# Sums of weight blocks: from VectorE additions with a store and a reload to transfers that add into the tile

## The chip, the cores and the metric

The kernel runs on one core of a Trainium2 chip. The time is what one execution takes on the device, in microseconds (us); before the change the median of two runs is 708.54 us (708.47 and 708.6). The profile is of one execution, recorded by the hardware.

The names used below are: TensorE (PE, the matmuls), VectorE (DVE), ScalarE (ACT), GpSimd (POOL) and SyncE (SP, which here only issues transfers). SPq and ACTq are the queues of transfers that SyncE and ScalarE issue. "L695" is line 695 of the kernel before.

## The reference

Two branches work on the same normalised input of 2048 rows and 512 columns, and their results are combined.

```
x  = A_x;  xn = layernorm(x)
s  = attention(xn @ wqkv: 32 heads of 16, each row sees 8 rows, 2 apart) @ wo
z  = gelu(xn @ w_in);  z1 = z[:, :896];  z2 = layernorm(z[:, 896:])
g  = w_sp @ z2 + b_sp            # w_sp is 2048 x 2048: it mixes the rows
b  = (z1 * g) @ w_out
out = x + s * silu(b)
```

What matters here is the product of the mixing weight `w_sp` with `z2` (2048 x 896). It is in float32.

## The kernel before

**Float32 on TensorE.** Each operand is split in a high part (written by ScalarE, L183) and a low part, the rest (written by VectorE, L184). A product of two blocks is three matmuls: high by high, high by low, low by high (`three`, L695). A weight block of 128 x 512 is loaded into a `raw` tile (SyncE's queue, L160), of which there are four, and split into one of eight pairs of high and low tiles (`prep`).

**The stages.** In the order of TensorE: qkv products (to about 110 us), the first half of `w_in` (z1), the second half with the layernorm (z2, 227 to 295), the mixing (295 to 583), the products with `w_out` (to 660) and with `wo` (to the end). The attention runs on VectorE in eight groups of heads. It has the lowest priority, so its steps are put wherever VectorE would have a gap, from z1 on to shortly before the products with `wo`.

**The mixing.** The output rows come in four groups of 512, called c. For c = 2 and 3 (295 to 447 us) all 16 blocks of `w_sp` are multiplied with `z2` as they are (line `PE g L695`). For c = 0 and 1 a scheme with fewer products is used on 3 of the 7 column blocks on either side (7 block products in place of 8): differences and sums of blocks of `z2` (`combine`, kept in `t_d`) are multiplied with sums of weight blocks. The seven are p1, p2, q6, q7, q5, q3 and q4, in this order, each by `block_product` over eight weight blocks, in four pairs. The middle column block (the "odd" one) is done without the scheme, beside p1, p2, q7 and q4. With `w[c, s]` for the block of output group c and input block s, and HT = 8, the sums are

- q6: `w[0,s] + w[1,s] + w[1,HT+s]`
- q7: `w[0,s] + w[1,s]`
- q5: `w[1,s] + w[1,HT+s]`
- q3: `w[0,s] + w[0,HT+s] + w[1,s] + w[1,HT+s]`

p1, p2 and q4 take a block as it is. Between the pairs of a product stand steps (`steps=`): loads and splits of the operands (`operand`: tiles `tr`), gate products (`upper_first` and others: `zl`) and splits of gated blocks of c = 2 and 3 (`late`: `ul`).

**Where the sums come from.** `block_sums(i)`, L557 to L569, makes all four for one s: two loads of 512 KB each (tiles `sa` and `sb`, L559 and L560), four additions on VectorE (L567), two stores of 512 KB into `sums_d` (L568 and L569, ScalarE's queue). It is called for i = 0 to 2 in the z1 loop and for i = 3 to 7 in the mixing of c = 2 and 3. q6, q7, q5 and q3 then load a block of sums like any other.

**What sets the order.** The kernel is written as a program in the order of the stages. The order of the instructions on each engine, except of those that are pinned to program order (the loads by L160 and the splits are), is chosen when it is built, by a scheduler which plays a model of the engines through. On the chip each engine works its own list in that order and waits, by semaphores, for what the next instruction needs. The transfers of one queue are issued in order too.

Of the kernel before, what the change touches and what calls it, by code (L numbers as in the profile page):

```python
# [11 lines left out]
F32 = mybir.dt.float32  # L12
F32R = mybir.dt.float32r
AF = mybir.ActivationFunctionType
ALU = mybir.AluOpType
AX = mybir.AxisListType

P = 128
# [6 lines left out]
FB = FH // P  # L25
NG = 3
CT = 512
NC = S // CT
JC = NT // NC
HT = NT // 2  # L30
# [16 lines left out]
RAW = 4  # L47
# [7 lines left out]
def kernel(  # L55
# [13 lines left out]
    nc = tc.nc  # L69
    pins = [True]  # L70

    def pin(ins):
        return tc.keep_in_program_order(ins) if pins[0] else ins
# [9 lines left out]
    raws = ctx.enter_context(tc.tile_pool(name="raws", bufs=1, side="right"))  # L83
# [3 lines left out]
    dram = ctx.enter_context(tc.tile_pool(name="scratch", bufs=1, space=DR))  # L87
# [3 lines left out]
    b_d = dram.tile([HT, P, 2, D], F32, name="b_d")  # L91
    z1_d = dram.tile([FB, NC, P, CT], F32, name="z1_d")
    g_d = dram.tile([2, FB, P, CT], F32, name="g_d")
    sums_d = dram.tile([2, HT, P, 2, CT], F32, name="sums_d")
    t_d = dram.tile([2, HT, P, 2, F3], F32, name="t_d")
    mv_d = dram.tile([NT, 2, P], F32, name="mv_d")
    o_d = dram.tile([NSUB, NT // NJ, CS, P // Q, NJ * Q], F32, name="o_d")
# [48 lines left out]
    def mm(name):  # L146
        return ps.tile([P, 512], F32, tag=f"bank{next(turn)}", name=name)
# [3 lines left out]
    def weight_pair(name):  # L151
        i = next(slot)
        return (
            wts.tile([P, 512], F32R, tag=f"whi{i}", name=name + "h"),
            wts.tile([P, 512], F32R, tag=f"wlo{i}", name=name + "l"),
        )

    def fetch(src, n, name):
        raw = raws.tile([P, 512], F32, tag="raw", name=name + "r", bufs=RAW)
        pin(nc.sync.dma_start(raw[:, :n], src))  # L160
        return raw

    def prep(src, n, name, raw=None):
        if raw is None:
            raw = fetch(src, n, name)
        hi, lo = weight_pair(name)
        split(hi[:, :n], lo[:, :n], raw[:, :n])
        return hi, lo

    @contextmanager  # L170
# [11 lines left out]
    def split(hi, lo, src):  # L182
        first_ = pin(nc.scalar.activation(hi, src, AF.Copy))  # L183
        pin(nc.vector.tensor_tensor(lo, src, hi.bitcast(F32), op=ALU.subtract))  # L184
        return first_
# [285 lines left out]
    def t4(name, n=2):  # L471
        t = wide.tile([P, 2 * CT], F32, tag="t4", name=name, bufs=WIDE)
        return t.rearrange("p (i t) -> p i t", i=2)[:, :n]
# [80 lines left out]
    for sub in range(NSUB):  # L554
        attention(sub)

    def block_sums(i):  # L557
        top, low = t4(f"sa_{i}"), t4(f"sb_{i}")
        nc.sync.dma_start(top, w_sp[0:2, i].rearrange("c p t -> p c t"))  # L559
        nc.sync.dma_start(low, w_sp[0:2, HT + i].rearrange("c p t -> p c t"))  # L560
        for out_, a, b in (
            (low[:, 1], top[:, 1], low[:, 1]),
            (top[:, 1], top[:, 0], top[:, 1]),
            (top[:, 0], top[:, 0], low[:, 1]),
            (low[:, 0], top[:, 0], low[:, 0]),
        ):
            nc.vector.tensor_tensor(out_, a, b, op=ALU.add)  # L567
        nc.scalar.dma_start(sums_d[0, i], top)  # L568
        nc.scalar.dma_start(sums_d[1, i], low)  # L569

    for f in range(FB):
        wh, wl = prep(w_in1[:, f, :], KB * P, f"w1_{f}")
        for c in range(NC):
            pz = mm(f"z1_{f}_{c}")
            for k in range(KB):
                cc = slice(k * P, (k + 1) * P)
                xh, xl = [planes[:, FB - KB + k, c * JC : (c + 1) * JC, a] for a in range(2)]
                nc.tensor.matmul(pz, wh[:, cc], xh, start=k == 0, stop=False)  # L578
                nc.tensor.matmul(pz, wh[:, cc], xl, start=False, stop=False)  # L579
                nc.tensor.matmul(pz, wl[:, cc], xh, start=False, stop=k == KB - 1)  # L580
            if c % 2 == 0:
                zp = t4(f"z1t_{f}_{c}")
            zt = zp[:, c % 2]
            if c == 0:
                nc.vector.tensor_tensor(zt, pz, rb, op=ALU.mult)
                pz = zt
            nc.scalar.activation(zt, pz, AF.Gelu_apprx_tanh)  # L587
            if c % 2:
                nc.scalar.dma_start(z1_d[f, c - 1 : c + 1].rearrange("c p t -> p c t"), zp)
        if f % 2:  # L590
            block_sums(f // 2)

    HALF = (slice(0, 512), slice(512, FH))
    WID = (512, FH - 512)
# [16 lines left out]
    def spatial_block(c, js):  # L611
        return prep(w_sp[c, js], CT, f"wsp_{c}_{js}")
# [55 lines left out]
    def bias(c):  # L668
        t = t4(f"bb_{c}")
        nc.sync.dma_start(  # L670
            t, b_sp[c : c + 2, :].rearrange("c t -> (c t)").unsqueeze(0).to_broadcast([P, 2 * CT])
        )
        return t
# [19 lines left out]
    def three(pg, z, w, start=False, stop=False, seeded=False):  # L693
        for i, (a, b) in enumerate(((0, 0), (0, 1), (1, 0))):
            nc.tensor.matmul(  # L695
                pg, z[a], w[b], start=start and i == 0, stop=stop and i == 2, skip_group_check=seeded
            )

    def z2_block(j, f):
        return [planes[:, f, j, a] for a in range(2)]  # L700
# [16 lines left out]
    for c in (2, 3):  # L717
        for n, js in enumerate(order):
            w = spatial.get((c, js)) or spatial_block(c, js)
            for f in range(FB):  # L720
                key = c, f
                three(banks[key], z2_block(js, f), w, n == 0 and key not in seeds, n == NT - 1, key in seeds)
            if n == HT:
                if c == 2:
                    banks[3, 0] = mm("g_3_0")
                else:
                    b01 = bias(0)
                    seed(("p", 0), "p1_0", b01[:, 0])
            if c == 2 and n % 4 == 0 or c == 3 and n == 5:
                block_sums(3 + n // 4 if c == 2 else 7)  # L730
        for f0 in range(0, FB, 2):
            n = min(2, FB - f0)
            zl = z1_pair(c, f0, n)
            gts = None if (c, f0 + n - 1) in seeds and f0 else t4(f"gt_{c}_{f0}", n)
            for f in range(f0, f0 + n):
                zt, src = zl[:, f - f0], banks[c, f]
                if (c, f) not in seeds:
                    gt = gts[:, f - f0]
                    nc.vector.tensor_tensor(gt, src, bb[:, c - 2], op=ALU.add)
                    src = gt  # L740
                nc.vector.tensor_tensor(zt, src, zt, op=ALU.mult)
                if c == 2 and f < FB - 1:
                    seed((3, f + 1), f"g_3_{f + 1}", bb[:, 1])
                if c == 3 and f < 3:
                    key = ("p", f + 1) if f < 2 else ("o", 0)
                    seed(key, f"p1_{f + 1}", b01[:, 0])
            nc.scalar.dma_start(g_d[c - 2, f0 : f0 + n].rearrange("f p t -> p f t"), zl)
# [11 lines left out]

    def block_product(name, key, z, w, odd=None, start=True, steps=()):  # L760
        for n, s0 in enumerate(range(0, HT, 2)):
            pair_ = [(s, prep(w(s), CT, f"{name}_{s}")) for s in (s0, s0 + 1)]
            for f in range(3):
                for s, wp in pair_:
                    three(
                        banks[key, f], z(s, f), wp, start and s == 0, s == HT - 1, not start
                    )
            if odd:
                for s, wp in pair_:
                    three(banks["o", odd[0]], odd[1](s), wp, False, s == HT - 1, True)  # L770
            for do in steps[n] if steps else ():
                do()
# [33 lines left out]
    def later(fn, *args):  # L806
        return lambda: fn(*args)
# [27 lines left out]

    T1, T2, T3, T4 = [[later(operand, i, h, s0) for s0 in range(0, HT, 2)] for i, h in ((0, 0), (1, 1), (1, 0), (0, 1))]

    block_product("p1", "p", upper, lambda s: w_sp[0, s], (0, odd_upper), start=False)
    ya, yb = t4("ya"), t4("yb")
    oq = t4("oq")  # L840
    yv, o1 = [ya[:, 0], ya[:, 1], yb[:, 0]], oq[:, 0]
    with urgent(400):
# [2 lines left out]
        nc.scalar.activation(o1, banks["o", 0], AF.Copy)  # L845
    nc.vector.tensor_tensor(b01[:, 1], b01[:, 0], b01[:, 1], op=ALU.add)
    block_product(
        "p2", "p", lower, lambda s: w_sp[0, HT + s], (0, odd_lower), start=False,
        steps=([], [T2[0]], [T2[1]], [T2[2]]),
    )  # L850
    fresh("q", "q6")
    block_product(
        "q6", "q", turned, lambda s: sums_d[0, s, :, 0],
        steps=(
            [T2[3], later(upper_first, 0)],
            [T3[0], later(upper_first, 2)],
# [6 lines left out]
    for f in range(3):  # L863
        seed(("q", f), f"q7_{f}", b01[:, 1], -1.0)
    seed(("o", 1), "o2", b01[:, 1])
    block_product(
        "q7", "q", turned, lambda s: sums_d[0, s, :, 1], (1, odd_upper), start=False,
        steps=([T3[3]], [T1[0]], [T1[1]], [T1[2], later(late, 2, 4, 1)]),
    )
    va, vb = t4("va"), t4("vb")  # L870
# [1 line left out]
    for f in range(3):  # L872
        minus(vv[f], yv[f], banks["q", f])
    fresh("q", "q5")
    block_product(
        "q5", "q", turned, lambda s: sums_d[1, s, :, 1],
        steps=([T1[3]], [later(late, 2, 5, 2)], [], []),
    )
    qv = [va[:, 1], vb[:, 1], oq[:, 1]]
    with urgent(400):  # L880
        for f in range(3):
            nc.scalar.activation(qv[f], banks["q", f], AF.Copy)
    block_product(
        "q3", "q", lambda s, f: z2_block(HT + s, FB - 3 + f), lambda s: sums_d[1, s, :, 0], start=False,
        steps=([T4[0], later(lower_last, 4, 2)], [T4[1], later(lower_last, 6, 1)], [T4[2]], [T4[3]]),
    )
    fresh("q4", "q4")
    block_product(
        "q4", "q4", turned, lambda s: w_sp[1, HT + s], (1, odd_lower), start=True,
        steps=(  # L890
            [later(upper_last, 4, 2)],
            [later(upper_last, 6, 1)],
# [23 lines left out]
    for i, j in enumerate(rows_of):  # L916
        c, jj = divmod(j, JC)
# [98 lines left out]
```

## Time and profile before

| | |
|---|---|
| median of 2 runs | 708.54 us |
| profiled execution: span | 706.6 us |
| runs' median less this span | 1.9 us |
| TensorE busy | 700.7 us (99% of the span) |
| VectorE busy | 619.2 us (88%) |
| ScalarE busy | 260.9 us (37%) |
| GpSimd busy | 41.8 us (6%) |
| moved by transfers | 151.93 MB, mean 215 GB/s |

The span goes from the first to the last instruction of the profiled execution; the time of a run has some more around it. The chain of waits is the work that ended last, followed back from the last instruction, at each step to what released it. A group of instructions is given with the number of them (x), the busy time and the mean of one. In the view of one tile it is the shortest, median and longest duration in ns. In the timeline each row has its start and its duration in us and, in square brackets, how long the engine was idle before it and what released it. Buffer numbers are left out of the tile names, so `q_4l` between 470 and 491 us is the low part of block 4 of q6, and `q_6r` the raw tile of a block 6.

### The profile page before, as it was taken

To read this page: it belongs to the slowest core of one execution; us is meant where nothing else is said; L and a number is where in the kernel's file an instruction comes from. 1 tells how busy PE (TensorE), PEld (TensorE's weight loads), DVE (VectorE), ACT (ScalarE), POOL (GpSimd) and SP (SyncE) were. 2 spreads that over 40 slices of the span, in tenths; PEclk is the share of its full clock that TensorE was granted. 3 is DMA by queue.
4 is the path that set the end of the run, shared out by engine and by line. 5 is a ranking of instruction groups with operands and counts; after the bars stand their busy time and mean duration, and the time that the engine had idled before them with its cause. 6 is when DMAs were issued, how large, how long until landed. Compare 5 with 4: busy or idle time off the path is not lost.

```text
span 706.6 us, 8920 instructions
## 1 busy us (share of the span) xinstructions
PE 700.7 (99%) x3152; PEld 585.4 (83%) x3152; DVE 619.2 (88%) x770; ACT 260.9 (37%) x403; POOL 41.8 (6%) x81
## 2 busy tenths in 40 slices
PE   8999999999999999999999999999999999999997
PEld 7888888888888988888888888888888888888886
DVE  6774599989998899989999999999999999799665
ACT  4343332343224466751112211354545542131531
POOL 3100000000000443320000000000000000000000
PEclk9999999999999999999999999999999999999999
DMA  8767775585785131579956742877857781353996
GB/s 271 255 189 228 240 242 178 161 287 207 258 275 220 33 135 69 190 255 323 328 183 219 288 135 60 307 239 260 276 200 269 246 260 59 125 165 101 303 327 235
DMA packets 96652, 151.93 MB, mean 215 GB/s; under 512 B 8672, under 2 KB 50912, under 8 KB 96608
## 3 DMA queue, kind: packets, MB, share of 16 engines
q1 hardware_dynamic: 57968, 108.77, 47.1%
q10 hardware_dynamic: 38640, 42.60, 17.3%
q8 instruction: 24, 0.39, 0.2%
q14 instruction: 20, 0.16, 0.1%
HBM read 100.40 MB, written 50.94 MB: 214 GB/s over the span
## 4 chain that ended last, share of the span: by engine, by line
PE 98%; DMA 1%; DVE 0%; SPq 0%; issue 0%
PE g L695 22%; PE q L695 12%; PE p L695 6%; PE qkv L371 6%; PE qkv L373 6%; PE qkv L372 6%; PE z L608 4%; PE z L607 4%; PE z L606 4%; PE z L580 4%; PE b L911 4%; PE z L578 4%; PE b L910 4%; PE b L912 4%; PE z L579 4%; PE s L911 2%
## 5 line engine op out<-in xcount | busy, mean ns | idle before, releaser
L503 DVE TENSOR_TENSOR pr<-k,q 128x2048 f32<-128x2048 f32 x32 | 73.2, 2286 | 1.9 <-DMA q<-qkv_d 1.5
L530 DVE TENSOR_TENSOR pv<-v,lg 128x2048 f32<-128x2048 f32 x32 | 73.3, 2291 | 0.9
L506 DVE TENSOR_REDUCE lg<-pr 128x128 f32<-128x2048 f32 x32 | 73.0, 2281 | 0.4
L391 ACT ACTIVATE stage<-qkv 128x512 f32<-128x512 f32 x36 | 21.4, 596 | 49.2 <-PE qkv L373 49.1
L536 DVE TENSOR_TENSOR pv<-pv 128x1024 f32<-128x1024 f32 x32 | 39.1, 1221 | 0.5
L608 PE MATMUL z<-w_0h,BIG 128*128 128x512 f32 x64 | 25.0, 391 | 0.0
L607 PE MATMUL z<-w_0l,BIG 128*128 128x512 f32 x64 | 25.0, 391 | 0.0
L606 PE MATMUL z<-w_0h,BIG 128*128 128x512 f32 x64 | 24.9, 389 | 0.0
L921 ACT ACTIVATE bt<-b 128x512 f32<-128x512 f32 x16 | 9.4, 597 | 41.5 <-PE b L912 41.5
L627 ACT ACTIVATE zt<-zt,nmz,mvz 128x896 f32<-128x896 f32 x16 | 17.9, 1134 | 17.6 <-POOL nmz L623 17.3
L267 DVE TENSOR_TENSOR xT<-xT,mr 128x512 f32<-128x512 f32 x20 | 13.8, 688 | 11.2 <-DMA mr<-mv_d 6.6
L537 DVE TENSOR_TENSOR pv<-pv 128x512 f32<-128x512 f32 x32 | 22.0, 687 | 0.6
L608 PE MATMUL z<-w_1h,BIG 128*128 128x384 f32 x64 | 21.5, 336 | 0.0
L606 PE MATMUL z<-w_1h,BIG 128*128 128x384 f32 x64 | 21.5, 335 | 0.0
L607 PE MATMUL z<-w_1l,BIG 128*128 128x384 f32 x64 | 21.4, 335 | 0.0
L587 ACT ACTIVATE z1t<-z 128x512 f32<-128x512 f32 x21 | 12.5, 594 | 21.8 <-PE z L580 21.8
L965 DVE TENSOR_TENSOR sg<-s,sg 128x512 f32<-128x512 f32 (+1 forms) x17 | 11.2, 657 | 10.6 <-PE s L912 9.7
L618 DVE BATCH_NORM_STATS2 zst<-zt 128x6 f32<-128x448 f32 x32 | 19.1, 610 | 1.5 <-ACT zt L609 1.5
L620 POOL TENSOR_TENSOR nmz<-mvz,mone 128x1 f32<-128x1 f32 x16 | 5.0, 315 | 234.8 <-DVE mvz L619 234.7
L184 DVE TENSOR_TENSOR BIG<-zt,BIG 128x896 fp32r<-128x896 f32 x16 | 17.1, 1079 | 1.1 <-ACT BIG L183 1.1
L609 ACT ACTIVATE zt<-z 128x512 f32<-128x512 f32 (+1 forms) x24 | 12.8, 535 | 13.4 <-PE z L608 12.1
L373 PE MATMUL qkv<-wqkv_0h,BIG 128*128 128x512 f32 x43 | 16.7, 389 | 0.0
(543 smaller groups left out, 2164.1 us busy)
## 6 DMA issues: line engine op xcount, KB each, us to landing
qkv_d<-stage ACTq DMA_DIRECT2D x24, 512.0 KB
k<-qkv_d SPq DMA_DIRECT2D x8, 960.0 KB
v<-qkv_d SPq DMA_DIRECT2D x8, 960.0 KB
z_d<-z1t ACTq DMA_DIRECT2D x14, 512.0 KB
t_d<-zt ACTq DMA_DIRECT2D x16, 384.0 KB
zl<-z_d SPq DMA_DIRECT2D x12, 512.0 KB
tr<-t_d SPq DMA_DIRECT2D x16, 384.0 KB
x<-in_x SPq DMA_DIRECT2D x16, 256.0 KB
```

The lines of the kernel that those rows point to most:

```text
L371: nc.tensor.matmul(pq, xh[:, k], wh, start=k == 0, stop=False)
L372: nc.tensor.matmul(pq, xh[:, k], wl, start=False, stop=False)
L373: nc.tensor.matmul(pq, xl[:, k], wh, start=False, stop=k == KB - 1)
L503: nc.vector.tensor_tensor(pr, taps(kw, j0), qb.unsqueeze(1).to_broadcast([P, W, NJ * CS]), op=ALU.mult)
L506: nc.vector.tensor_reduce(lg[:, :, j0 * HS : (j0 + NJ) * HS], pr.rearrange("p w (i d) -> p w i d", d=DH), axis=AX.X, op=ALU.add,)
L530: nc.vector.tensor_tensor(pr.rearrange("p w (i d) -> p w i d", d=DH), taps(vw, j0).rearrange("p w (i d) -> p w i d", d=DH), lg[:, :, j0 * ...
L536: nc.vector.tensor_tensor(pr[:, 0:4], pr[:, 0:4], pr[:, 4:8], op=ALU.add)
L606: nc.tensor.matmul(pz, xh[:, k], wh, start=k == 0, stop=False)
L607: nc.tensor.matmul(pz, xh[:, k], wl, start=False, stop=False)
L608: nc.tensor.matmul(pz, xl[:, k], wh, start=False, stop=k == KB - 1)
L695: nc.tensor.matmul(pg, z[a], w[b], start=start and i == 0, stop=stop and i == 2, skip_group_check=seeded)
L911: nc.tensor.matmul(pp[:, cols], hi, wl, start=False, stop=False)
```

## The change

`block_sums` and `sums_d` go, with the calls. `prep_sum` takes a list of blocks: the first is loaded into the raw tile by SyncE's queue, and each of the others is added to it by a transfer which GpSimd's queue issues with `accum_op=ALU.add`. After that the tile is split as before. p1, p2 and q4 have lists of one block. Compared with `prep`, the load and the split are no longer both pinned: the load in `prep_sum` isn't, the split is.

```diff
-    sums_d = dram.tile([2, HT, P, 2, CT], F32, name="sums_d")
...
+    def prep_sum(srcs, name):
+        hi, lo = weight_pair(name)
+        raw = raws.tile([P, 512], F32, tag="raw", name=name + "r", bufs=RAW)
+        nc.sync.dma_start(raw, srcs[0])
+        for src in srcs[1:]:
+            nc.gpsimd.dma_start(raw, src, accum_op=ALU.add)
+        split(hi, lo, raw)
+        return hi, lo
...
-    def block_sums(i):
-        top, low = t4(f"sa_{i}"), t4(f"sb_{i}")
-        nc.sync.dma_start(top, w_sp[0:2, i].rearrange("c p t -> p c t"))
-        nc.sync.dma_start(low, w_sp[0:2, HT + i].rearrange("c p t -> p c t"))
-        for out_, a, b in (
-            (low[:, 1], top[:, 1], low[:, 1]),
-            (top[:, 1], top[:, 0], top[:, 1]),
-            (top[:, 0], top[:, 0], low[:, 1]),
-            (low[:, 0], top[:, 0], low[:, 0]),
-        ):
-            nc.vector.tensor_tensor(out_, a, b, op=ALU.add)
-        nc.scalar.dma_start(sums_d[0, i], top)
-        nc.scalar.dma_start(sums_d[1, i], low)
...
-        if f % 2:
-            block_sums(f // 2)
...
-            if c == 2 and n % 4 == 0 or c == 3 and n == 5:
-                block_sums(3 + n // 4 if c == 2 else 7)
...
-            pair_ = [(s, prep(w(s), CT, f"{name}_{s}")) for s in (s0, s0 + 1)]
+            pair_ = [(s, prep_sum(w(s), f"{name}_{s}")) for s in (s0, s0 + 1)]
...
-    block_product("p1", "p", upper, lambda s: w_sp[0, s], (0, odd_upper), start=False)
+    block_product("p1", "p", upper, lambda s: [w_sp[0, s]], (0, odd_upper), start=False)
...
-        "q6", "q", turned, lambda s: sums_d[0, s, :, 0],
+        "q6", "q", turned, lambda s: [w_sp[0, s], w_sp[1, s], w_sp[1, HT + s]],
...
-        "q7", "q", turned, lambda s: sums_d[0, s, :, 1], (1, odd_upper), start=False,
+        "q7", "q", turned, lambda s: [w_sp[0, s], w_sp[1, s]], (1, odd_upper), start=False,
...
-        "q5", "q", turned, lambda s: sums_d[1, s, :, 1],
+        "q5", "q", turned, lambda s: [w_sp[1, s], w_sp[1, HT + s]],
...
-        "q3", "q", lambda s, f: z2_block(HT + s, FB - 3 + f), lambda s: sums_d[1, s, :, 0], start=False,
+        "q3", "q", lambda s, f: z2_block(HT + s, FB - 3 + f), lambda s: [w_sp[0, s], w_sp[0, HT + s], w_sp[1, s], w_sp[1, HT + s]], start=False,
```

p2 and q4 are changed as p1 is.

More of the change, by code (lines that the diff above doesn't have):

```diff
@@ L847 @@
     block_product(
-        "p2", "p", lower, lambda s: w_sp[0, HT + s], (0, odd_lower), start=False,
+        "p2", "p", lower, lambda s: [w_sp[0, HT + s]], (0, odd_lower), start=False,
         steps=([], [T2[0]], [T2[1]], [T2[2]]),
@@ L888 @@
     block_product(
-        "q4", "q4", turned, lambda s: w_sp[1, HT + s], (1, odd_lower), start=True,
+        "q4", "q4", turned, lambda s: [w_sp[1, HT + s]], (1, odd_lower), start=True,
         steps=(
```

## The prediction

> **What bounds the kernel now.** I read the head and the chain of waits first, then the busy time by stretch.
>
> ```profile
> span 706.6 us, 8920 instructions
> PE 700.7 (99%) x3152; PEld 585.4 (83%) x3152; DVE 619.2 (88%) x770; ACT 260.9 (37%) x403; POOL 41.8 (6%) x81
> PE 98%; DMA 1%; DVE 0%; SPq 0%; issue 0%
> ```
>
> TensorE is busy for 700.7 of 706.6 us and is 98% of the chain. Whatever is taken from another engine can win back at most 706.6 − 700.7 = 5.9 us, under 1%. The change can lose much more, wherever a weight block comes later than TensorE wants it. The stretches that use the sums are q6, q7, q5 and q3, with q4 behind them; the first two rows are stretches in which the sums are made (columns: stretch, its us, then busy us and instructions of PE, PEld, DVE, ACT, POOL, the granted clock, the DMA share, GB/s):
>
> ```profile
> 61.00:227.00 166.00, 166.00 (x740) 138.17 (x739) 141.98 (x137) 57.78 (x93) 0.00 (x0) 1.00 0.69 230
> 295.00:447.00 152.00, 152.00 (x673) 125.81 (x672) 144.16 (x169) 36.83 (x54) 6.62 (x14) 1.00 0.67 230
> 491.00:507.00 16.00, 16.00 (x72) 13.27 (x71) 16.00 (x19) 9.83 (x17) 0.00 (x0) 1.00 0.75 237
> 507.00:529.00 22.00, 22.00 (x98) 18.22 (x98) 22.00 (x28) 9.78 (x15) 0.00 (x0) 1.00 0.64 215
> 529.00:545.00 16.00, 16.00 (x72) 13.23 (x72) 15.09 (x18) 7.80 (x14) 0.00 (x0) 1.00 0.83 294
> 545.00:561.00 16.00, 16.00 (x72) 13.24 (x71) 16.00 (x24) 9.72 (x17) 0.00 (x0) 1.00 0.72 230
> 561.00:583.00 22.00, 22.00 (x99) 18.21 (x98) 21.25 (x32) 10.87 (x19) 0.00 (x0) 1.00 0.81 257
> ```
>
> From 491 on VectorE is as full as TensorE, since attention fills every gap, and GpSimd is idle. The chain gives the price of a matmul and the borders:
>
> ```profile
> 447.16 43.52 PE p L695 x192
> 490.68 20.40 PE q L695 x90
> 528.76 36.72 PE q L695 x162
> ```
>
> 43.52/192 = 0.2267 us each. A pair of blocks is 18 matmuls, 4.08 us, in q6, q5 and q3, and 24, 5.44 us, in q7 and q4, which have the odd column too. q6 starts at 490.68, right at p2's end; this is my zero below. Four pairs each make q6 16.3, q7 21.8, q5 16.3, q3 16.3 and q4 21.8 us.
>
> **What the change removes.** The views of the tiles sa and sb:
>
> ```profile
> L567 DVE TENSOR_TENSOR sb<-sa,sb x16: 650/686/694, 165.9 to 394.1; 128x512 f32<-128x512 f32 x16
> L567 DVE TENSOR_TENSOR sa<-sa x8: 675/685/693, 167.4 to 390.1; 128x512 f32<-128x512 f32 x8
> L560 SPq DMA_DIRECT2D sb<-in_w_sp x8: 367/379/1248, 154.4 to 380.9; - x8
> L569 ACTq DMA_DIRECT2D sums_d<-sb x8: 327/354/803, 172.7 to 394.9; - x8
>   ACT wsp_0h L183: 6.3, 1
> ```
>
> Eight calls of four additions are 32 × 0.686 = 22.0 us of VectorE; with them go 16 loads and 16 stores of 512 KB and one 6.3 us wait of ScalarE. All lie before 396 us, in stretches where TensorE is busy for 166.00 of 166 and 152.00 of 152 us: worth 0 on the chain. What VectorE gains is filled with attention, which would have been done later.
>
> **What it adds: 56 accumulating transfers.** q6 needs two per block, q7 and q5 one, q3 three: 16 + 8 + 8 + 24, each 256 KB. Before, such a block was one load from the sums. Issue on SyncE's queue, and the ScalarE split that this load released:
>
> ```profile
> 503.06 0.41 SPq L160 DMA_DIRECT2D q_6r<-sums_d  x1
> 515.89 0.32 SPq L160 DMA_DIRECT2D q_3r<-sums_d  x1
> 532.00 0.38 SPq L160 DMA_DIRECT2D q_2r<-sums_d  x1
> 554.24 0.34 SPq L160 DMA_DIRECT2D q_4r<-in_w_sp  x1
> 508.76 0.64 ACT L183 ACTIVATE q_6h<-q_6r 128x512 fp32r<-128x512 f32 x1 [2.40 <-DMA q_6r<-sums_d]
> 518.65 0.64 ACT L183 ACTIVATE q_3h<-q_3r 128x512 fp32r<-128x512 f32 x1 [0.79 <-DMA q_3r<-sums_d]
> 539.02 0.63 ACT L183 ACTIVATE q_2h<-q_2r 128x512 fp32r<-128x512 f32 x1 [4.93 <-DMA q_2r<-sums_d]
> 558.45 0.64 ACT L183 ACTIVATE q_4h<-q_4r 128x512 fp32r<-128x512 f32 x1 [1.26 <-DMA q_4r<-in_w_sp]
> ```
>
> 5.70, 2.76, 7.02 and 4.21 us from issue to use: mean 4.92. No accumulating transfer is in this trace. I bound one by the same size of load, 2.76 from below and 7.02 from above, and take 4.92, the mean in just these stretches. It moves the same bytes on the same, 64 to 83% busy, DMA engines, and nothing here says that adding is cheaper than copying.
>
> [...]
>
> Now the chain. The built order of the changed kernel has the transfers of one tile strictly one behind the other, each released by the one before. GpSimd's queue is in order too, alternating between the two blocks of a pair, so both come at about the same time. There are four raw buffers, so two pairs are under way, and a buffer is free for its next load only when VectorE has split its block. With load l, addition a, m additions, and about 2 us for the two splits with their turn on ScalarE and VectorE (0.64 above and 0.6 below, twice, less the overlap, rounded up for the wait in line), pairs come every (l + m·a + 2)/2:
>
> - q6 (m = 2): (4.92 + 9.84 + 2)/2 = 8.38 us for 4.08 of products. The order has only q6's first pair split ahead of p2's end (before, six blocks were, below). I take the second to be just in time, as its chain is under way by then. Two late pairs: 2 × 4.30 = **8.6**.
> - q7 (m = 1): 5.92 against 5.44, 4 × 0.48 = **1.9**.
> - q5 (m = 1): 5.92 against 4.08, 4 × 1.84 = **7.4**.
> - q3 (m = 3): 10.84 against 4.08. The built order puts q4's blocks 0 to 3 ahead of q3's last pair on TensorE. Count from T, when q5's last pair is ready: q3's last pair is ready at T + 43.4. VectorE splits it behind q4's block 3, whose load waits in line behind q4's first pair: T + 46. TensorE then still has 5.44 + 4.08 + 10.88, so q4 ends at T + 66.4. Unhindered it would be T + 4.08 + 16.3 + 21.8 = T + 42.2. Loss **24**.
>
> Together 42 us.
>
> **What the order on VectorE adds.** It is in order, and the split of a block is now placed among attention steps and others that wait for p2's end. Before, blocks 4 and 5 of q6 were split five us ahead of that end, as these rows of the VectorE timeline show (start, us); the rest give the pitches:
>
> ```profile
> 484.17 1.23 DVE L536 TENSOR_TENSOR pv<-pv 128x1024 f32<-128x1024 f32 x1
> 485.31 0.68 DVE L184 TENSOR_TENSOR q_4l<-q_4r,q_4h 128x512 fp32r<-128x512 f32 x1
> 485.94 0.69 DVE L184 TENSOR_TENSOR q_5l<-q_5r,q_5h 128x512 fp32r<-128x512 f32 x1
> 497.30 2.28 DVE L506 TENSOR_REDUCE lg<-pr 128x128 f32<-128x2048 f32 x1
> 499.49 0.95 DVE L184 TENSOR_TENSOR BIG<-tr,BIG 128x768 fp32r<-128x768 f32 x1
> 500.36 0.69 DVE L184 TENSOR_TENSOR q_1l<-q_1r,q_1h 128x512 fp32r<-128x512 f32 x1
> 546.44 1.09 DVE L523 TENSOR_REDUCE sm<-lg 128x64 f32<-128x512 f32 x1
> 547.44 0.69 DVE L804 TENSOR_TENSOR oq<-yb,oq 128x512 f32<-128x512 f32 x1
> 551.05 0.55 DVE L524 RECIPROCAL sm<-sm 128x64 f32<-128x64 f32 x1
> 551.51 0.63 DVE L794 TENSOR_TENSOR zl<-oq,zl 128x512 f32<-128x512 f32 x1
> ```
>
> Start to start: 2.19 us for 2048 wide, 1.14 for 1024, 0.87 for 768, 0.60 for 512, 1.00 for the short reduction, 0.46 for a reciprocal (also used for the transpose; 0.36 for its 256-wide input). In the changed order, the steps from the first gate product (`zl <- p_0`, which needs p2's first bank, complete some 3.4 us before p2's end) to the split of q4's last block come to 110.7 us with no wait at all. So that split ends no earlier than 110.7 − 3.4 = 107.3 after zero. Unhindered, TensorE would be done with q4 at 16.3 + 21.8 + 16.3 + 16.3 + 21.8 = 92.5, and behind the split it has about 2.7 us left: **the order alone costs 110.0 − 92.5 = 17.5**, with transfers that cost nothing. It isn't added to the 42, since the chains fill the same time (T is 54.4 + 17.9 − 4.08 = 68.2 after zero, so they bring q3's last split to 114, against 97 by the order alone). Where a finished pair still stands behind a 2.19 us step (q5's block 7 has two of them ahead, q3's first block stands behind q5's results) I add 3. That makes 45.
>
> Nothing behind q4 pays it back. The last stretch holds little idle time on TensorE:
>
> ```profile
> 615.00:706.00 91.00, 87.99 (x400) 73.17 (x398) 64.84 (x76) 28.29 (x40) 0.00 (x0) 1.00 0.67 220
> ```
>
> 3.0 us, of which the final output is part: 0 to −1, left out. **Sum:** 706.6 + 45 = 751.6 for the profiled execution; the median of the runs before lies 708.54 − 706.6 = 1.9 above its span, so **753.5 us**.
>
> **Rivals.**
>
> *B: the additions are dearer than loads.* [...] At 7.02 us for load and addition the spacings are 11.5, 8.0, 8.0 and 15.0; by the same steps 15 + 10 + 16 + 43 + 3 = +87. With only the additions dearer by one 2.19 us VectorE step (7.11) it is 13 + 6 + 12 + 37 + 3 = +71. So 780 to 796. [...] Against: the mean row is shorter.
>
> [...]
>
> *C: only VectorE's order counts.* With additions of 2.76 us or less the chain terms (q6 4, q5 1, q3 some 11) stay under the order's 17.5, and together they give +18 to +27: 726 to 736.
>
> *D: the additions run one at a time,* over all tiles. 56 × 2.76 = 155 or 56 × 4.92 = 276 us against 70.7 us of q6, q7, q5 and q3, less some 25 that the first ones start ahead: +59 to +180, 767 to 889. Against: GpSimd's queue waits only for a tile's own buffer.
>
> *E, the other side: the read-ahead hides it.* Eight weight pairs and four raw buffers let blocks come early. If all transfers are in time, and TensorE gets back its 5.9 us of idle time against the order's 17.5, the sum is +11.6: 720; if VectorE's steps are shorter too, nothing is lost: 703 to 722. It decides if q6's block 6 is split by some 15 us after zero, when TensorE comes to it. For it: GpSimd is free from 447 on. Against: the split order, which by the pitches above has it at 20.2 whatever the transfers do.
>
> *F: the change doesn't do what it says* would mean that no transfer adds: then only the loads are left, which is C's or E's time.
>
> **How the numbers follow.** Forecast A (735 to 775) 0.50; B (780 to 796) 0.20; C 0.13; D 0.08; E 0.08; faster by over 2% 0.01, because TensorE's 700.7 us excludes it. A measurement of this kernel can tell about 2%, 14 us, from no change; E is all that lies within it, at 722.7 or less. Range for 8 in 10: from 722 over C, A and B into D's beginning, 815.
>
> **What would show it.** On TensorE, idle time from q6 to q4 of some 45 us, near 9 in q6, 24 in q3 and q4, with waits of ScalarE's high split or TensorE for an accumulating transfer; additions of about 5 us from issue to landing, and pairs about 8.4, 5.9, 5.9 and 10.8 us apart. Waits named after VectorE's low split alone speak for C. Additions over 7 us speak for B, additions that never overlap for D, TensorE full in 491 to 583 for E. I am wrong if idle time appears ahead of 447, or if additions to two tiles wait for each other.

## The result and the profile after

The changed kernel takes 776.26 us (773.89 and 778.64), 1.0956 times the kernel before (95% interval 1.0877 to 1.1035). The forecast was 753.5 with a range of 722 to 815. The direction and the range hold; the loss is half as large again as forecast: 771.8 − 706.6 = 65.2 us of span, against 45. The medians differ by 67.7 us. The two runs here and the four of `space_2048` below, which has the same order of instructions, lie between 773.85 and 779.85 us, so single runs of this kernel spread over 6 us.

The head of the page of the changed kernel, the chain of waits by engine, and its transfers by queue (q0 is GpSimd's: packets, MB, share of sixteen engines' span):

```profile
span 771.8 us, 8916 instructions
PE 722.0 (94%) x3152; PEld 593.9 (77%) x3152; DVE 603.2 (78%) x738; ACT 263.6 (34%) x405; POOL 92.2 (12%) x137
q0 software_dynamic: 8064, 14.68, 11.3%
PE 77%; DMA 14%; DVE 4%; issue 2%; ACT 1%; POOL 1%; SPq 0%; POOLq 0%; ACTq 0%; DVEq 0%
```

Two things are to be seen. TensorE idles for 771.8 − 722.0 = 49.8 us in place of 5.9. And it is busy for 722.0 us in place of 700.7, with the same 3152 matmuls. The windows say where (columns as in the prediction; the last four rows are q6, q7, q5 with the wait for q3's first block, and q3 with q4):

```profile
61.00:227.00 166.00, 166.00 (x740) 138.17 (x739) 142.30 (x131) 58.01 (x93) 0.00 (x0) 1.00 0.59 193
295.00:447.00 152.00, 152.00 (x672) 125.83 (x671) 141.28 (x156) 37.82 (x57) 6.16 (x8) 1.00 0.49 166
490.40:523.50 33.10, 21.16 (x73) 15.66 (x73) 25.63 (x35) 13.20 (x23) 8.19 (x10) 0.85 1.02 280
523.50:547.70 24.20, 22.75 (x98) 17.81 (x97) 17.21 (x24) 8.13 (x12) 8.55 (x10) 1.00 0.88 191
547.70:587.80 40.10, 23.70 (x74) 15.67 (x72) 29.65 (x32) 10.08 (x16) 11.52 (x14) 0.77 0.99 246
587.80:648.00 60.20, 45.62 (x168) 35.52 (x169) 43.12 (x55) 19.88 (x33) 13.72 (x16) 0.84 0.83 188
```

Up to p2's end, at 490.4, nothing has changed for TensorE, though VectorE is rid of its 32 additions. Then q6 takes 33.1 us (16.3 before), q7 24.2 (21.8), q5 40.1 (16.3), q3 and q4 60.2 (38.1): 16.8 + 2.4 + 23.8 + 22.1 = 65.1 us more. From 648 on TensorE does what it did before from 583 on. What TensorE waits for in the changed kernel, from the list of waits (us in all, times, longest):

```profile
PE q L687 <- ACT q_4h L191: 15.8, 2, 8.7
PE q L687 <- ACT q_0h L191: 9.5, 2, 8.3
PE q L687 <- ACT q_2h L191: 5.5, 2, 4.5
PE q L687 <- ACT q_6h L191: 4.1, 1, 4.1
PE q L687 <- DVE q_6l L192: 2.9, 1, 2.9
```

The longest are for a high split, which ScalarE makes within 0.1 us of the landing of the tile's last transfer (in one block 2.1 us after it); VectorE's low split comes far behind. One block of q6 through its chain, from the timelines of SyncE, GpSimd, ScalarE and TensorE (start, us, what, in brackets the idle time before and its releaser):

```profile
482.35 0.34 SPq L172 DMA_DIRECT2D q_4r<-in_w_sp  x1
489.77 0.88 POOL L174 DMA_DIRECT2D q_4r<-in_w_sp  x1 [0.55 <-issue]
497.93 0.88 POOL L174 DMA_DIRECT2D q_4r<-in_w_sp  x1 [5.76 <-DMA q_4r<-in_w_sp]
506.04 0.61 ACT L191 ACTIVATE q_4h<-q_4r 128x512 fp32r<-128x512 f32 x1
506.70 1.65 PE L687 MATMUL q<-q_4h,BIG 128*128 128x512 f32 x3 [7.12 <-ACT q_4h L191]
```

7.4, 8.2 and 8.1 us for a load and two additions, and TensorE waits for the split that follows. I had 4.92 for each. The 8.2 are the first addition itself: GpSimd idles for 5.76 us until it has landed, 7.8 us after its issue by the trace. Of the 8.1, 2.1 are ScalarE's: this is the block whose data had landed while ScalarE was still at other steps of its order. The same over all eight blocks of a product, as means worked out from these timelines:

| | load to first addition | addition to next | last addition to high split | both splits | a block in all |
|---|---|---|---|---|---|
| q6 | 6.4 | 8.1 | 6.6 | 1.6 | 22.7 |
| q7 | 5.5 | | 5.3 | 1.5 | 12.3 |
| q5 | 5.3 | | 6.7 | 2.3 | 14.3 |
| q3 | 9.1 | 6.2 | 5.1 | 1.4 | 28.0 |

Four buffers hold eight blocks of each: (22.7 + 12.3 + 14.3 + 28.0) × 8/4 = 154.6 us, and from q6's first load (464.8) to q3's last split (631.5) there are 166.7. With q4's first four blocks, which are loaded and split within this time (24.8 us together, 6.2 in four buffers), it is 161. The buffers are occupied almost without a break.

### The profile page after: what moved, and what is told of

It is laid out like the page before. It is cut to its first block, busy times and chain, and to the rows that moved or that the text cites. A ratio compares the mean times of both kernels' runs of the same rounds, so it can differ in the third digit from the quotient of the medians.

```text
span 771.8 us, 8916 instructions
## 1 busy us (share of the span) xinstructions
PE 722.0 (94%) x3152; PEld 593.9 (77%) x3152; DVE 603.2 (78%) x738; ACT 263.6 (34%) x405; POOL 92.2 (12%) x137
## 3 DMA queue, kind: packets, MB, share of 16 engines
q0 software_dynamic: 8064, 14.68, 11.3%
## 4 chain that ended last, share of the span: by engine, by line
PE 77%; DMA 14%; DVE 4%; issue 2%; ACT 1%; POOL 1%; SPq 0%; POOLq 0%; ACTq 0%; DVEq 0%
PE g L687 20%; PE qkv L379 5%; PE qkv L380 5%; PE qkv L381 5%; DMA q_4r<-in_w_sp 4%; PE z L600 3%; PE z L599 3%; PE z L598 3%; PE z L572 3%; PE b L901 3%; PE b L900 3%; PE z L573 3%; PE z L574 3%; PE b L902 3%; PE p L687 3%; DMA q_2r<-in_w_sp 3%
## 5 line engine op out<-in xcount | busy, mean ns | idle before, releaser
L612 POOL TENSOR_TENSOR nmz<-mvz,mone 128x1 f32<-128x1 f32 x16 | 8.4, 524 | 233.9 <-DVE mvz L611 233.8
L687 PE MATMUL q<-q_4h,BIG 128*128 128x512 f32 x30 | 13.5, 475 | 15.8 <-ACT q_4h L191 15.8
L174 POOL DMA_DIRECT2D q_0r<-in_w_sp x7 | 6.6, 941 | 172.2 <-DMA q_1r<-in_w_sp 158.3
L955 DVE TENSOR_TENSOR sg<-s,sg 128x512 f32<-128x512 f32 (+1 forms) x17 | 11.2, 659 | 16.1 <-PE s L902 15.2
L275 DVE TENSOR_TENSOR xT<-xT,mr 128x512 f32<-128x512 f32 x20 | 13.8, 688 | 11.2 <-DMA mr<-mv_d 6.4
L192 DVE TENSOR_TENSOR o_1l<-ol,o_1h 128x512 fp32r<-128x512 f32 x3 | 2.1, 689 | 26.1 <-ACT o_1h L191 26.1
L619 ACT ACTIVATE zt<-zt,nmz,mvz 128x896 f32<-128x896 f32 x16 | 17.9, 1134 | 11.7 <-POOL nmz L615 11.7
L687 PE MATMUL q<-q_0h,BIG 128*128 128x512 f32 x30 | 12.4, 447 | 9.5 <-ACT q_0h L191 9.5
```

Source lines behind the costliest of these rows:

```text
L687: nc.tensor.matmul(pg, z[a], w[b], start=start and i == 0, stop=stop and i == 2, skip_group_check=seeded)
```

## The experiments

Every run is compared with runs of the kernel before on the same chip (708.1 to 708.4 us).

**How many additions.** First without any, then with at most one per block.

```diff
-        for src in srcs[1:]:
+        for src in srcs[1:1]:      # loads_only;  srcs[1:2]: one_add
```

> The changed kernel without its 56 additions: each block of q6, q7, q5 and q3 is only the first of its list (the sums are left out). Theory (the transfers in series on a raw buffer set the pace): with one load of some 5 us and 2 us for the splits a pair comes every (5 + 2)/2 = 3.5 us, under the 4.08 of products, and the built order on VectorE allows q4's last split at 73 us after q6 begins, under 92.5: nothing is lost, 703 to 713 us. Rival (something else of the change, as the freed attention or the sums' absence before 447 us, costs time): above 715.

> The changed kernel with at most one addition per block in q6, q7, q5 and q3 (32 in place of 56; q6 and q3 lack the rest of their sums). Theory with the measured prices (load to first addition 5.4, addition to split 6, splits 2 us): a pair every 6.7 us; q6 2 x 2.6, q7 4 x 1.3, q5 4 x 2.6, q3 and q4 some 8: 29 us over the kernel before, 732 to 745. If the loss went with the number of additions alone, it would be 68 x 32/56 = 39, 747.

Without additions 708.42 us, 1.0002 times the kernel before (0.9992 to 1.0012), with TensorE as full as it was:

```profile
PE 700.7 (99%) x3152; PEld 585.4 (83%) x3152; DVE 601.3 (85%) x738; ACT 263.3 (37%) x405; POOL 42.6 (6%) x81
```

So the whole loss hangs on the additions, with the order that is built around them, and the 22 us that VectorE saves are worth nothing, as forecast. With 32 additions it is 740.6 us (1.0452, 1.0433 to 1.047), inside the span forecast from the chain, and below the 747 of a loss by count alone.

**What an addition costs.** Plain copies in their place, and additions of an eighth of the bytes.

```diff
-            nc.gpsimd.dma_start(raw, src, accum_op=ALU.add)
+            nc.gpsimd.dma_start(raw, src)                                        # copies
+            nc.gpsimd.dma_start(raw[:, :64], src[:, :64], accum_op=ALU.add)      # small_adds
```

> The changed kernel with its 56 accumulating transfers turned into plain copies from the same GpSimd queue into the same tiles (the sums are left out; each copy overwrites the tile). The order on every engine is that of the changed kernel, and each transfer still waits for the one before it on its tile. Theory (the serial chain of transfers and the four raw buffers set the pace, whatever a transfer does): 765 to 785 us, issue to landing still 5.4 to 6.2 us in the middle. Rival (adding is what makes them dear): well below, toward 735, with the copies at 4 us or less from issue to landing.

> The changed kernel with each accumulating transfer cut from 512 to 64 columns (256 KB to 32 KB; most of the sums is left out). The count of transfers and of waits is the same; the built order on VectorE changes and would alone allow q4's last split at 91.6 - 3.4 = 88.2 us after q6 begins, so it costs nothing by itself (92.5 is TensorE's own). If a transfer's price is mostly fixed (issue, start, the release of the next wait), an addition stays at 4 us or more and the time at 745 to 770 us. If the price is bytes on DMA engines that are 0.9 to 1.0 busy, an addition falls to some 2.5 us and the time to 715 to 735.

The copies give 747.33 us (1.0554, 1.0529 to 1.058), between the two expectations: with each instruction in the same place, **adding costs 29 us more than copying**. The lists of transfers, first the changed kernel's, then that of the copies (tile, count, KB each, median us from issue to landing), and the queue's row of the copies:

```profile
q_0r<-in_w_sp POOLq DMA_DIRECT2D x7, 256.0 KB, 6.0
q_3r<-in_w_sp POOLq DMA_DIRECT2D x7, 256.0 KB, 5.6
```

```profile
q_0r<-in_w_sp POOLq DMA_DIRECT2D x7, 256.0 KB, 4.0
q_3r<-in_w_sp POOLq DMA_DIRECT2D x7, 256.0 KB, 4.3
q0 software_dynamic: 4480, 14.68, 5.9%
```

For the same 14.68 MB the additions keep the DMA engines for 11.3% of 771.8 = 87 us of sixteen engines' time, the copies for 5.9% of 747.9 = 44, and there are 8064 packets in place of 4480. Whether the adding itself or the larger number of packets makes the difference isn't separated here. The small additions give 737.12 us (1.0403, 1.0387 to 1.0419), also between the two expectations. Their rows:

```profile
q_0r<-in_w_sp POOLq DMA_DIRECT2D x7, 32.0 KB, 3.8
q_3r<-in_w_sp POOLq DMA_DIRECT2D x7, 32.0 KB, 3.2
```

An eighth of the bytes still takes 3.2 to 3.8 us of 5.6 to 6.0: the larger part of an addition's price doesn't go with the bytes. Its packets are as many as before (8064), so whether it goes with the transfer or with its packets is open. The loss is still 28.8 us, but not all of it is the chain's: the order is another here, and TensorE's longest wait, 6.4 us, is for ScalarE's copy of q5's result.

**Does TensorE's low clock count?** Behind each of the changed kernel's six waits of 2.9 to 8.7 us the matmuls start at about half their pace, 0.43 us from start to start, and behind five of them this lasts 3.1 to 5.7 us (behind the sixth, of 2.9 us, the next waits come first). These rows of its TensorE timeline follow the 7.12 us wait above:

```profile
510.43 0.63 PE L687 MATMUL q<-q_4h,BIG 128*128 128x512 f32 x1
510.85 0.63 PE L687 MATMUL q<-q_5h,BIG 128*128 128x512 f32 x1
...
512.33 0.39 PE L687 MATMUL q<-q_5h,BIG 128*128 128x512 f32 x1
512.55 0.39 PE L687 MATMUL q<-q_5l,BIG 128*128 128x512 f32 x1
```

0.42 us from start to start, and from 511.6 on, 4.9 us after the restart, 0.22. This is where the 21.3 us of longer busy time come from (the granted clock is 0.85, 0.77 and 0.84 in the rows of q6, q5 and q3 with q4 above). By arithmetic they and the added idle time, 49.8 − 5.9 = 43.9, make the 65.2; and 43.9 is so close to the forecast 45 that I took the clock for the missing part. Two runs test it: one fills the waits with matmuls that nobody uses, the other leaves out a third of the matmuls in q6, q5 and q3.

```diff
+    def fill(wp, n):
+        for i in range(n):
+            nc.tensor.matmul(filler["bank"], z2_block(0, 0)[0], wp[0], start=True, stop=True)
...
+            fill(pair_[1][1], FILL.get((name, n), 0))    # filler: behind the pair's products
...
-                    three(
+                    (two if name in ("q6", "q5", "q3") else three)(    # fewer_matmuls
```

> The changed kernel, with 176 extra matmuls (40 us at 0.2267 us each) into an unused bank, placed where TensorE waits for the next pair in q6, q5 and q3 (34 and 18 in q6, 16, 12 and 30 in q5, 30 and 36 in q3); results are unchanged. TensorE was idle for 49.8 us and busy for 21.3 us more than before, since its clock is granted at 0.67 to 0.85 in the stretches with long waits. Theory (each wait of some us costs a second time, because the matmuls behind it run at the low clock): the extra matmuls lie in the waits and hold the clock up, 752 to 768 us, with a granted clock near 1.00 from 491 to 660. Rival (the low clock isn't due to the waits, or the extra work delays the products): the same time or more, 775 to 815.

> The changed kernel with the third matmul (low part of the operand by high part of the weights) left out in q6, q5 and q3: 72 matmuls fewer, 16.3 us at 0.2267 us each, more at the low clock; all transfers are kept. It tells whether TensorE's own work, with its low clock after a wait, is on the path of the loss. Theory (supply alone sets the pace; a slower TensorE only waits less): 768 to 778 us, idle time up by about what is left out. Rival (the 21.3 us by which TensorE was busy longer are lost beside the waits): 745 to 760.

`filler`: 789.91 us (1.1155, 1.1138 to 1.1172), against what I expected. The clock did rise, from 0.86 in the first of these rows (the changed kernel) to 0.92 in the second, not to 1.00:

```profile
490.00:660.00 170.00, 125.63 (x464) 94.96 (x463) 128.01 (x162) 54.72 (x90) 42.38 (x48) 0.86 0.91 225
```

```profile
491.00:660.00 169.00, 138.66 (x567) 109.97 (x567) 119.86 (x147) 49.99 (x82) 42.42 (x48) 0.92 0.88 210
```

It doesn't settle the matter, since the extra matmuls also moved instructions of the other engines. `fewer_matmuls` has another order too, so it is no clean test either. It takes 782.11 us (1.1042, 1.1018 to 1.1065), 4 us more than the theory's 778 and no faster with 72 matmuls less, far from the rival's 745 to 760. TensorE is busy for 707.2 of 780.9 us, so its idle time is 73.7 in place of 49.8:

```profile
span 780.9 us, 8778 instructions
PE 707.2 (91%) x3080; PEld 580.8 (74%) x3080; DVE 602.9 (77%) x738; ACT 263.6 (34%) x405; POOL 92.5 (12%) x137
PE q L752 <- ACT q_6h L191: 17.2, 3, 9.8
```

(the last row is from the list of waits: us in all, times, longest). What TensorE doesn't compute it waits. The chain of waits of the changed kernel itself says more. These are the last piece of TensorE in it before the stretch, and the pieces with which TensorE comes back (start, us, what, instructions):

```profile
447.08 21.09 PE p L687 x93
628.99 0.64 ACT q_3h L191
629.67 1.89 PE q L687 x7
```

Between 468.2 and 629.7 us the chain holds no matmul, only transfers, splits and steps of the other engines, as the profile infers them. **The low clock is real, but it isn't on the path here**: a raw buffer comes free when VectorE has split its block, whether TensorE is done with it or not, so the supply goes on at its own pace while TensorE works slowly. My reading by arithmetic falls.

**More buffers, then more in flight, then cheaper transfers.** Eight raw buffers (room: six wide tiles in place of eight), and apart from that, and together with it, `dynamic_dma_scratch_size` at 2048 in place of 1024.

```diff
-RAW = 4
+RAW = 8          # raw8, raw8_space_2048, raw8_copies
-WIDE = 8
+WIDE = 6
...
-    nc = _bacc.Bacc("TRN2", target_bir_lowering=False, num_devices=1, dynamic_dma_scratch_size=1024)
+    nc = _bacc.Bacc("TRN2", target_bir_lowering=False, num_devices=1, dynamic_dma_scratch_size=2048)
```

> The changed kernel with eight raw buffers in place of four (room is made by six of the wide tiles in place of eight), all 56 additions kept. Four pairs are under way in place of two. Theory (buffers times chain length set the pace): spacing (l + m a + 2)/4 with l = 5 and a = 5.7 gives 4.6 for q6, 3.2 for q7 and q5 and 6.0 for q3; loss 1 + 8, with a few us of clock and start, 712 to 728 us. Rival (the DMA engines, 0.9 to 1.0 busy from 491 to 620, are the limit, or additions of different tiles go one at a time): little changes, 755 to 780.

> The changed kernel with dynamic_dma_scratch_size=2048 in place of 1024 in the line that creates the program; the order on every engine is the same. In the kernels run so far GpSimd is often idle ahead of a transfer without any wait that the profile shows (the releaser is called issue): after one transfer of 512 KB for 7 to 9 us, with eight raw buffers 1 to 4 us after three of 256 KB. If the setting limits what is in flight, these gaps shrink; in the changed kernel itself they come to only some 6 us, so little is won: 765 to 777. Rival (the limit slowed every transfer of the changed kernel): 745 to 760.

> The kernel with eight raw buffers (750.9 us) and dynamic_dma_scratch_size=2048 in place of 1024; the order on every engine is the same. Theory (there some three transfers of 256 KB are in flight at most, 56 of them in 130 us, 2.3 us each, and that is the pace): the gaps called issue go, 715 to 738. Rival (the DMA engines, at 1.04 to 1.09 by the profile's share from 491 to 588, are the limit): no change, 745 to 755, and the single transfer gets longer than 6.9 us.

> The kernel with eight raw buffers and dynamic_dma_scratch_size=2048 (745.2 us), with its 56 accumulating transfers turned into plain copies (the sums are left out); the order on every engine is the same. In it the DMA engines are at 1.09 to 1.11 by the profile's share from 491 to 588 and an addition takes 8.5 to 10 us. As copies the same bytes took 5.9% of sixteen engines' span of 747.9 us, 44 us, and as additions 11.3% of 771.8, 87 us. Theory (with room for eight blocks the DMA engines' time is the limit, and adding takes twice as much of it): 43 us less of sixteen engines' time among some 130 us, so 712 to 725 us, share under 1.0. Rival (what is left is order and waits of other engines): 736 to 748.

`raw8` gives 750.9 us (1.0595, 1.0577 to 1.0612): 25 us come back, in another order, not the 50 that I expected. GpSimd's timeline shows a first limit. After three additions in a row the fourth is held back with no wait that the profile names, and the gaps of this kind come to 38.1 us in all (by the trace's landings never more than three are in flight):

```profile
462.23 1.08 POOL L174 DMA_DIRECT2D q_0r<-in_w_sp  x1 [148.44 <-DVE tt L553]
463.01 1.21 POOL L174 DMA_DIRECT2D q_1r<-in_w_sp  x1
463.71 1.42 POOL L174 DMA_DIRECT2D q_2r<-in_w_sp  x1
467.30 0.89 POOL L174 DMA_DIRECT2D q_3r<-in_w_sp  x1 [2.17 <-issue]
```

With 2048 the fourth goes out with the others, and the gaps are down to 0.5 us (up to seven are in flight):

```profile
463.15 1.56 POOL L174 DMA_DIRECT2D q_2r<-in_w_sp  x1
464.47 1.14 POOL L174 DMA_DIRECT2D q_3r<-in_w_sp  x1
```

In the changed kernel itself 2048 makes no difference (`space_2048`: 777.26 us, 1.0973, 1.0933 to 1.1013). With eight buffers it is worth 6 us (745.16 us, 1.0518, 1.0501 to 1.0536), which is the rival's expectation: an addition takes 7.0 to 10.0 us now. The second limit is seen in the DMA share, the number before the last, from 491 to 588, with `raw8_space_2048` first and `raw8_copies` second:

```profile
491.00:588.00 97.00, 73.21 (x278) 55.78 (x276) 74.83 (x91) 31.69 (x53) 37.27 (x42) 0.88 1.10 278
```

```profile
491.00:588.00 97.00, 91.01 (x389) 73.52 (x388) 92.14 (x113) 39.53 (x65) 20.18 (x37) 0.98 0.88 308
```

I take 1.10 as full; no stretch read here is above 1.11. The copies in the same places bring it to 0.88 while more GB/s are moved, and the time to 718.4 us (1.014, 1.0121 to 1.0158). So behind the chain stands the doubled engine time of an addition (87 us against 44 for all 56), and other transfers take longer beside it: TensorE's longest wait in `raw8_space_2048`, 10.2 us, isn't for a block of weights but for an operand, whose load was issued at 556.36 and let ScalarE split it only 11.0 us later (in the kernel before, the last such load was issued at 553.04 and split at 556.35, 3.3 us later):

```profile
567.34 0.84 ACT L191 ACTIVATE BIG<-tr 128x768 fp32r<-128x768 f32 x1 [11.73 <-DMA tr<-t_d]
```

**Off the path.** Now the sums as before, ahead of 470 us and with stores and reloads, but made by accumulating transfers; then with the stores on GpSimd's queue.

```diff
-        for out_, a, b in (
-            (low[:, 1], top[:, 1], low[:, 1]),
...
-            nc.vector.tensor_tensor(out_, a, b, op=ALU.add)
+        nc.sync.dma_start(top, twice(w_sp[0, i]))
+        nc.sync.dma_start(low, twice(w_sp[1, HT + i]))
+        nc.gpsimd.dma_start(top, twice(w_sp[1, i]), accum_op=ALU.add)
+        nc.gpsimd.dma_start(low, twice(w_sp[1, i]), accum_op=ALU.add)
+        nc.gpsimd.dma_start(top[:, 0], w_sp[1, HT + i], accum_op=ALU.add)
+        nc.gpsimd.dma_start(low[:, 0], w_sp[0, HT + i], accum_op=ALU.add)
+        nc.gpsimd.dma_start(low[:, 0], w_sp[0, i], accum_op=ALU.add)
-        nc.scalar.dma_start(sums_d[0, i], top)     # early_2: nc.gpsimd, both stores
```

> The kernel before, with its sums made early as there (the same calls, the same tiles sa and sb, the same stores and reloads), but by accumulating transfers from GpSimd's queue in place of VectorE's four additions: two loads that fill both halves of a tile and five accumulating transfers per call, 40 in all, moving the seven block additions of the sums. Results are those of the kernel before. Theory (what costs is the place, in series ahead of the split; an accumulating transfer that nobody waits for costs nothing): 703 to 713 us, TensorE busy for some 701. Rival (such transfers cost by themselves, through the DMA engines or GpSimd's queue, wherever they are): above 715.

> The kernel early (759.5 us) with the stores of the sums on GpSimd's queue in place of ScalarE's, and dynamic_dma_scratch_size=2048. There TensorE waited 31.5 us once for a seed that ScalarE writes, and ScalarE's z1 step 33.6 us for the tile sb: a store stands on ScalarE's queue until the slow chain of its tile ends, and what ScalarE has to do next stands behind it. Theory (only this blocked, the transfers themselves cost nothing where nobody waits): 704 to 716. Rival (the additions load the DMA engines so that the loads for the mixing come late, or the sums come too late for q6): 720 to 750.

`early` is a miss: 759.54 us (1.0725, 1.0705 to 1.0746). q6 to q4 run without a wait, but TensorE idles before. ScalarE's timeline shows why: the store of a sum stands in its queue until the slow additions of its tile are done, and a split that TensorE needs stands behind the store:

```profile
378.94 0.64 ACT L183 ACTIVATE wsp_2h<-wsp_2r 128x512 fp32r<-128x512 f32 x1 [0.67 <-DMA wsp_2r<-in_w_sp]
408.38 0.33 ACTq L571 DMA_DIRECT2D sums_d<-sb  x1
411.35 0.33 ACTq L570 DMA_DIRECT2D sums_d<-sa  x1
411.80 0.63 ACT L183 ACTIVATE wsp_10h<-wsp_10r 128x512 fp32r<-128x512 f32 x1 [32.22 <-DMA sa<-in_w_sp]
```

32.22 us of ScalarE's idle time, and about as much of TensorE's in one wait behind it, by its list of waits:

```profile
PE g L697 <- ACT g L716: 31.5, 1, 31.5
```

`early_2`, with the stores elsewhere, gives 729.47 us (1.0301, 1.0284 to 1.0319): 30 us come back, yet not all. TensorE still idles for 13 us where the sums of the mixing stage are made, with the DMA engines at 0.95, against 0.67 in the kernel before:

```profile
295.00:447.00 152.00, 139.05 (x587) 113.57 (x586) 132.47 (x155) 43.99 (x64) 43.05 (x57) 0.94 0.95 283
```

In the chain of waits the wait of 6.6 us at 384 to 390 goes back to a plain load of a weight block that took 15.1 us, while the 6.3 us of two waits between 295 and 308 go back, over ScalarE's and GpSimd's steps of the layernorm, to VectorE's, in an order of this kernel's own. Another 5.6 us are longer busy time of TensorE (706.3 us in place of 700.7). That the load on the DMA engines makes up all of what is left was not tried by itself. No version with accumulating transfers reached the kernel before.

## Why the prediction was right, and where not

- **Removed: worth 0.** Right: TensorE is at 166.00 of 166 and 152.00 of 152 us before and after, and `loads_only` takes the time of before.
- **Form of the added cost: transfers in series on four buffers.** Right: `loads_only` and `one_add` follow it, the buffers are occupied for 154.6 of 166.7 us, and the chain of waits holds no matmul from 468 to 630. With the measured totals of a block in place of l + m·a + 2, the prediction's steps give 14.5 (q6) + 2.8 (q7) + 12.3 (q5) + 36.8 (q3 and q4) = 66 us, against 65. The time, 776, lies between the ranges of A (to 775) and B (from 780) and is in the stated range only because that is wide.
- **Price of an addition, 4.92 us, "nothing here says that adding is cheaper than copying".** This is the term that was mis-sized. That adding could be dearer than a load was left to a rival, priced from the longest load. By tile, copies from the same queue take 3.3 to 5.5 us in the median (six of eight tiles 4.0 to 4.6), additions 5.4 to 6.2. In the sum of the prediction, 5.6 in place of 4.92, with a load of 5, gives (5 + 11.2 + 2)/2 = 9.1 for q6, 6.3 for q7 and q5 and 11.9 for q3: 10 + 3 + 9 + 28 + 3 = 53 in place of 45. With 4.4, for the copies, it gives 8 + 1 + 6 + 21 + 3 = 39, and they lost 747.33 − 708.31 = 39.0. That this is exact is luck: with the copies' own totals of a block (19.8, 10.7, 12.0 and 23.0 us) the steps give 46.
- **The rest, 65 − 53 = 12,** I read in the same table. In q6 the additions themselves were dearer than the medians over all products say: by the trace's landings 7.7 us for the first and 6.3 for the second in the mean, with the next transfer of the tile out 0.4 us behind the landing. In q3 a block's load took 9.1 us to its first addition. For blocks 6 and 7 (11.7 and 12.8 us) GpSimd's queue, in order, held the last additions of blocks 4 and 5 ahead. I had written down that the queue is in order, and then let two pairs run side by side. For q5's block 7, which waited 11.4 us, it was SyncE's queue: its load stands behind the attention's load `v`, as these rows of SyncE's and GpSimd's timelines show; in the chain of waits `v` takes 9.93 us, to 565.1. The releaser named in the last row is one of several semaphores, and I read the wait as that for the load.

```profile
555.21 0.48 SPq L499 DMA_DIRECT2D v<-qkv_d  x1
556.27 0.35 SPq L172 DMA_DIRECT2D q_7r<-in_w_sp  x1
567.65 0.89 POOL L174 DMA_DIRECT2D q_7r<-in_w_sp  x1 [9.87 <-DVE tt L553]
```

- **By products:** q6 16.8 (forecast 8.6), q7 2.4 (1.9), q5 to q4 45.9 (7.4 + 24 + 3 = 34.4).
- **The constant 0.2267 us per matmul** was wrong behind each wait of 2.9 us and more: 0.42 us from start to start for 4.9 us after the wait of 7.12 us. In the changed kernel it cost nothing, by the chain; in `early_2`, where TensorE goes on without further waits, I estimate that the 5.6 us of longer busy time are lost.
- **Rivals.**
  - B (additions dearer than loads) is right in part: the first additions of q6 took over 7 us, its own sign, and the DMA engines are at 1.02 in q6. With VectorE's order unchanged, turning additions into copies took 29 us away. The VectorE step of 2.19 us by which its second sum makes an addition dearer is shown by no run: GpSimd issues in 0.88 us also in the midst of a step of VectorE (at 553.48, in one of 2.29 us from 552.16), and additions took 5.4 to 6.2 us in the median by tile, where that sum has 7.11.
  - C as the only cause is excluded, since the copies have the same order and are 29 us faster, and the waits name the high split and thus a transfer. But VectorE isn't off the path: in the chain of waits the stretch from 551.55 to 585.24 runs over VectorE's steps and two loads. That VectorE's order alone costs 17.5 was not tried, as every run that lightened the transfers enough had another order. C's sum has a slip: by the prediction's formula q5 loses 4 × (4.84 − 4.08) = 3 at 2.76 us, not 1, which puts the chain level with the order's 17.5.
  - D is excluded: in `raw8` the second addition goes out to another tile at 463.01, and the first lands only at 467.0.
  - E is excluded: the windows show 12 us of idle time in q6 alone.
  - F is excluded: GpSimd's queue moves the 14.68 MB of 56 transfers, in other packets than the copies.
- **An error of the description:** it says that loads and splits are pinned to program order. The switch for this is off throughout the mixing stage, so the scheduler places them all; no number rests on it.

## What to carry to other kernels

A buffer's chain counts with all its transfers: pace = (load + additions + split) × blocks / buffers, and where that is above the consumer's time, as here (buffers occupied for 154.6 of 166.7 us), the consumer's own speed no longer matters. The order of other work counts in it as well: a load that stands behind a larger one in its queue holds its buffer for that time (11.4 us for q5's block 7). Before additions are moved from an idle-enough engine to transfers, price the accumulating transfer by itself, in us and in DMA engine time, against a copy (5.4 to 6.2 us against 3.3 to 5.5 here, 87 us of sixteen engines against 44). And a store that waits for such a chain must not stand on the queue of an engine which something urgent needs (in `early` ScalarE idled for 32.22 us ahead of a split).

## What the runs showed of the hardware that I had not expected

- An accumulating transfer kept the DMA engines about twice as long as a copy of the same bytes (87 against 44 us of sixteen engines for 14.68 MB).
- Its price goes little with its bytes: 3.1 to 4.0 us from issue to landing for 32 KB, 5.4 to 6.2 for 256 KB (medians by tile), with as many packets.
- In `raw8`, with `dynamic_dma_scratch_size=1024`, no more than three transfers of 256 KB were in flight from GpSimd's queue, and in `early` GpSimd idled for 7.1 to 8.9 us between the first transfer of 512 KB and the next; with 2048 the gaps were gone (38.1 to 0.5 us in all with eight buffers).
- Half the matmul pace (0.42 us from start to start in place of 0.22) for 4.9 us after a wait of 7.12 us, without cost in the changed kernel, where supply is the limit.
